# Loading the first four heads of Q and K in f32 through the SP and ACT queues and casting them on the chip

## The chip, the cores and the metric

The kernel runs on one core of one Trainium2 chip. The metric is device time in microseconds (us), the median of several executions of one compiled program. All repeated runs quoted here were undisturbed ("fast").

The names used below are these. PE (or TensorE) does matmuls, PEld is its weight load, DVE is VectorE, ACT is ScalarE, POOL is GpSimd, and SP is SyncE. A DMA that Pool issues can cast f32 to bf16 on the way ("Pool's queue"). A DMA issued by SP or ACT goes through a hardware queue and, in this kernel, brings f32, which an engine must cast afterwards.

## The reference

Attention with a squared ReLU (8 batches, 12 heads, 448 positions, head size 64), then RMS norm and a SwiGLU feed-forward layer over 3584 tokens (768 to 1536 to 768).

```python
def _attn_ref(q, k, v):                       # each (8, 12, 448, 64), f32
    scores = np.matmul(q, k.transpose(0, 1, 3, 2)) / np.sqrt(64)
    attn = np.maximum(scores, 0.0) ** 2 / 448
    return np.matmul(attn, v)

def _moe_ref(x, w_gate, w_val, w_out, rms_g): # x: (3584, 768)
    xn = x / np.sqrt(np.mean(x * x, axis=-1, keepdims=True) + 1e-06) * rms_g
    g = xn @ w_gate
    return (g / (1.0 + np.exp(-g)) * (xn @ w_val)) @ w_out
```

## The kernel before

The kernel is written by its own planner. While the program is built, `Planner` keeps a rough model of each engine's clock and of the DMA landings. At each step it emits whatever it believes can start next. What results is a fixed order of instructions for each engine, and each engine executes its list in order. Waits on real data are correct however wrong the model was; only the order is frozen.

Q and K have to be transposed on TensorE before the scores (tile `psT`). They come from DRAM by Pool's queue, four heads at a time; a DMA moves two chunks of Q, or one of two halves of K:

```python
def load_q(b, h0, h1, c0=0, c1=NCH):
    t = new_ld("q", b)                                  # bf16
    def go():
        nc.gpsimd.dma_start(out=t[:, h0:h1, c0*D:c1*D], in_=q[b, h0:h1].rearrange(...))
    landed("q", b, h0, h1, issue(go, ...))              # issue(): the planner's model of the DMA
...
def load_k(b, h0, h1):
    load_runs("k", b, h0, h1, low, 0, UH)               # partitions 0..63, 1024 B of f32 each
    load_runs("k", b, h0, h1, high, UH, U)              # partitions 64..127, 768 B each
```

The order of loads at the start:

```python
nc.scalar.preload_act_table_set(NORM_SET)
nc.sync.dma_start(out=g_sb[:], in_=moe_rms_g.rearrange("(kt p) -> p kt", p=P))
load_q(0, 0, 4, 0, 2)
load_k(0, 0, 4)
identTok = pl.task(-1, {"pool": 550.0}, lambda e: masks.make_identity(nc, ident[:]) and None)
load_q(0, 4, 8, 0, 2)
load_k(0, 4, 8)
load_v(0, 0, 4)
load_q(0, 8, H, 0, 2)
load_k(0, 8, H)
load_v(0, 4, H)
load_q(0, 0, H, 2, 4)
load_w(0, 2)                                            # first gate and value weights
...
```

Where the planner believes that PE has nothing to do for over 250 ns before the feed-forward part begins, it emits a filler: a matmul of constants into a bank that nobody reads (`psB`). The first ones warm TensorE up: in the profile of the kernel before they start 187 ns apart at first and 96 ns apart from about 5.5 us on.

```python
if self.warm() and (not times or min(times) > t + 250.0):
    return t, self.filler
...
def fill():
    ...
    nc.tensor.matmul(out=bank.fill, lhsT=ones_bf[:], rhs=busy_bf[:], start=True, stop=True)
    cost = 96.0 if max(pl.t) > pl.WARM else 189.0
```

Of the kernel before, what the change touches and what calls it, by code (L numbers as in the profile page):

```python
# [13 lines left out]
NCH = 4  # L14
U = 7
# [39 lines left out]
class Planner:  # L55
# [6 lines left out]
    def __init__(self, nc, tc, banks, wide, warm):  # L62
        self.nc, self.tc, self.banks, self.wide, self.warm = nc, tc, banks, wide, warm
        self.free = {"act": 1300.0, "dve": 1500.0, "pool": 1300.0, "sp": 1300.0}
        self.tasks, self.seq = [], 0
        self.t = [1100.0, 1100.0]
        self.mode = "row"
        self.ins = [[], []]
        self.aux = None
        self.cur, self.next0, self.q8 = None, [], []  # L70
        self.stream = []
        self.units, self.auxes, self.sneaks = [], [], []
        self.behind = mybir.DependencyInfo(
            mybir.DependencyClass.Sync, mybir.DependencyReason.DATA
        )
# [8 lines left out]
    def engine_next(self):  # L84
        best = None
        for item in self.tasks:
            prio, seq, cost, emit, need, out, then = item
            r = latest(need)
            if r is None:
                continue  # L90
            for e in cost:
                s = max(r, self.free[e])
                if e == "pool" and len(cost) > 1:
                    s += self.SLOW
                key = (s, prio, seq)
                if best is None or key < best[0]:
                    best = (key, item, e, s)
        return best
# [234 lines left out]
def kernel(  # L333
# [24 lines left out]
    PE_T = 2  # L358
    R = 14
    PACE = 0.93  # L360

    ctx.enter_context(tc.manual_schedule())

# [4 lines left out]
    apool = ctx.enter_context(tc.tile_pool(name="attn", bufs=R))  # L368
    xpool = ctx.enter_context(tc.tile_pool(name="xT", bufs=2))
    npool = ctx.enter_context(tc.tile_pool(name="norm", bufs=1))  # L370
    hpool = ctx.enter_context(tc.tile_pool(name="hT", bufs=1))
    spool = ctx.enter_context(tc.tile_pool(name="sig", bufs=3))
    opool = ctx.enter_context(tc.tile_pool(name="ostage", bufs=3))
    psum = ctx.enter_context(tc.tile_pool(name="psum", bufs=1, space=bass.MemoryType.PSUM))

    early = ExitStack()
    psum_x = early.enter_context(tc.tile_pool(name="psum_x", bufs=1, space=bass.MemoryType.PSUM))
# [6 lines left out]
    def act_cost(n, per=0.8333):  # L384
        return 172.0 + per * n

    def dve_cost(n, per=1.0417):
        return 156.0 + per * n
# [45 lines left out]
    def new_ld(nm, b):  # L434
        if (nm, b) not in ld:
            n, w = (PC, NCH) if nm == "q" else (P, UH)
            runs = nm == "v" or b < PE_T
            shape = [n, H, w * D] if runs else [n, w, H * D]
            ld[nm, b] = ldpool.tile(shape, BF16, name=nm + "b", tag=nm + "b")
            if nm == "k" and runs:  # L440
                nc.vector.memset(ld[nm, b][D:, :, (UH - 1) * D :], 0.0)
            ldtok[nm, b] = {}
        return ld[nm, b]

# [108 lines left out]
    def transposes(b, pairs, c0, c1, with_k, gate=lambda: True):  # L553
# [24 lines left out]
        def run(s):  # L578
# [18 lines left out]
            def copy(e):  # L597
                if with_k:
                    dst = t[:, pairs[0]].rearrange("p t s -> p (t s)")[:, c0 * PC : c0 * PC + width]
                    src = ps[:, :width]  # L600
                else:
                    dst = t[:, pairs[0] : pairs[-1] + 1, 1, c0 * PC : c1 * PC]
                    src = ps[:, :width].rearrange("p (j s) -> p j s", s=n)
                if e == "dve":
                    nc.vector.tensor_copy(out=dst, in_=src)
                else:
                    nc.scalar.copy(out=dst, in_=src)

            pl.task(
                2, {"dve": dve_cost(width, 0.52), "act": act_cost(width)}, copy, [Tok(end + 200.0)],  # L610
                done, free_bank(bank),
            )
            return end

        pl.auxes.append(Aux("transposes", "col", ready, run))

# [152 lines left out]
    def visit_aux(sub, k, then, after):  # L769
# [36 lines left out]
        def run(s):  # L806
# [38 lines left out]
            sub.visited = k + 1  # L845
            if (b, 0) not in xTs:
                xTs[b, 0] = xpool.tile([P, KT, S], BF16, name="xT", tag="xT")
                if b == 0:
                    x2s[b] = npool.tile([P, KT, S], BF16, name="x2", tag="x2")
                else:  # L850
                    accs[b] = npool.tile([P, S], FP32, name="acc", tag="acc")
                    x2s[b] = npool.tile([P, S], BF16, name="ssum", tag="ssum", bufs=2)
# [6 lines left out]
                else:  # L859
                    nc.vector.tensor_scalar_mul(out=xT[at], in0=ps[:, :, :n], scalar1=inv_attn)  # L860

            c = pl.task(1, {"act": act_cost(2 * n), "dve": dve_cost(2 * n)}, copy, [told], None, free_bank(bank))
            if b == 0:
                def squared(e):
                    nc.vector.tensor_tensor(out=x2s[b][at], in0=xT[at], in1=xT[at], op=ALU.mult)

# [45 lines left out]
    def norm_sum(sub):  # L912

        b, n, got = sub.b, sub.n, {}

        def ready():
            r, f = latest([sub.sum]), bank_ready()
            return None if r is None or f is None else max(r, f)

        def half(h):  # L920
            prt = (low, high)[h]
            if h:
                pl.wait_for(got["mm"])
            got["mm"] = nc.tensor.matmul(  # L924
                out=got["tile"][:, :n], lhsT=ones_bf[prt], rhs=x2s[b][prt], start=h == 0, stop=h == 1,
            ).ins

        def run():
            got["bank"] = take_bank()
            got["tile"] = got["bank"].take("psSS")  # L930

            def first(t):
                pl.ins[1].append((n, lambda: half(1), lambda t: norm_scale(sub, got, t), t - pl.PSUM + pl.HAND))

            pl.ins[0].append((n, lambda: half(0), first, 0.0))

        return Aux("sums", "row", ready, run)

    def norm_scale(sub, bk, ready):
# [5 lines left out]
        table["now"] = "silu"  # L945

        def power(e):
            if switch:
                nc.scalar.preload_act_table_set(NORM_SET)
            nc.scalar.activation(  # L950
# [12 lines left out]
        )]  # L963
        for kt in range(KT):
            def scale(e, kt=kt):
                if b not in xns:
                    xns[b] = npool.tile([P, KT, S], BF16, name="xn", tag="xn")
                xn = xns[b]
# [41 lines left out]
    def ffn_seg(sublist, w_nm, fbs):  # L1010
# [13 lines left out]
        def done(bk, ready):  # L1024
# [11 lines left out]
            else:  # L1036
                o = (b % 2) * S + q0

                def hidden(e):
                    if b // 2 not in hTs:  # L1040
                        hTs[b // 2] = hpool.tile([P, FT, 2 * S], BF16, name="hT", tag="hT")
                    h = hTs[b // 2]
                    s = sil[b, q0, fbs[0]][0]
                    nc.vector.tensor_tensor(  # L1044
# [108 lines left out]



    nc.scalar.preload_act_table_set(NORM_SET)
    nc.sync.dma_start(out=g_sb[:], in_=moe_rms_g.rearrange("(kt p) -> p kt", p=P))

    load_q(0, 0, 4, 0, 2)
    load_k(0, 0, 4)  # L1160
    identTok = pl.task(-1, {"pool": 550.0}, lambda e: masks.make_identity(nc, ident[:]) and None)
    load_q(0, 4, 8, 0, 2)
    load_k(0, 4, 8)
    load_v(0, 0, 4)
    load_q(0, 8, H, 0, 2)
    load_k(0, 8, H)
    load_v(0, 4, H)
    load_q(0, 0, H, 2, 4)
    load_w(0, 2)
    load_w(2, 4)  # L1170
# [16 lines left out]

    for j in range(HP):
        transposes(0, [j], 0, 2, True)
    for j in range(0, HP, 3):  # L1190
        transposes(0, [j, j + 1, j + 2], 2, 4, False, gate=lambda: begun(a0) >= 6)
    for j in range(HP):
        transposes(
            1, [j], 0, 4, True,
            gate=lambda j=j: begun(a1) >= 6 if j < 2 else begun(subs[2]) >= 3 * (j - 2),
        )


    period = 2 * FT * KT * (S / 2.4 + 2.5)

    def due_of(sub, i, total):
        if not sub.pace:
            return lambda: True

# [124 lines left out]
```

## Time and profile before

| | before |
|---|---|
| time, median (first three runs) | 441.01 us (440.78 to 441.23) |
| first transposes start | 6.44 us |
| first gate matmul (`psg`) starts | 25.19 us |
| span of the profiled run | 438.5 us |

The page of the kernel before. The first line is busy time, share of the span and count by engine. The second and third are PE's busy tenths and the granted TensorE clock in 40 slices of the span. The last is the chain of waits that ended last, by engine.

```profile
PE 432.1 (99%) x5443; PEld 302.4 (69%) x5443; DVE 272.0 (62%) x444; ACT 246.0 (56%) x345; POOL 79.7 (18%) x100
PE   8999999999999999999999999999999999999996
PEclk9999999999999999999999999999999999999999
PE 94%; DVE 2%; DMA 1%; ACT 1%; POOL 1%; issue 1%; ACTq 0%; POOLq 0%
```

PE is busy almost throughout, so from some point on only less PE work could help. The first 25 us are different, as the timeline shows. Its columns are start, duration, engine, line, operation, tiles, shape and count; in brackets stands how long the engine had been idle and for what.

```profile
1.18 5.13 PE L1278 MATMUL psB<-busy_bf,ones_bf 128*128 128x224 bf16 x30 [1.18 <-DVE busy_bf L397]
1.31 0.84 POOL L454 DMA_DIRECT2D qb<-in_q_dram  x1 [0.86 <-POOLq L1313]
2.13 1.25 POOL L466 DMA_DIRECT2D kb<-in_k_dram  x2
...
6.44 0.41 PE L590 MATMUL psT<-ident,kb 128*64 128x128 bf16 x8
6.66 0.29 PE L590 MATMUL psT<-ident,qb 112*64 112x112 bf16 x4
...
25.19 0.73 PE L139 MATMUL psg<-xn,wg_sb 64*128 64x224 bf16 x6
```

TensorE runs 30 fillers until Q and K have come, the transposes start at 6.44 us, and eight of them take 0.41 us.

The DMA view of the first 12 us, in slices of 0.3 us; an issue line ends with the size and the us from the start of the issue to the landing (the median, where it stands for several).

```profile
GB/s 0 0 0 0 0 0 3 5 3 22 49 112 157 149 182 144 150 78 107 106 159 120 132 141 114 139 106 111 115 134 152 164 172 167 162 171 178 173 183 160
qb<-in_q_dram POOLq DMA_DIRECT2D x3, 112.0 KB, 4.5
kb<-in_k_dram POOLq DMA_DIRECT2D x3, 128.0 KB, 4.5
kb<-in_k_dram POOLq DMA_DIRECT2D x3, 96.0 KB, 4.4
g_sb<-in_moe_rms_g_dram SPq DMA_DIRECT2D x1, 3.0 KB, 2.2
```

Pool's loads take about 4.5 us from issue to landing, as the median of three; the first ones, of heads 0 to 3, took 3.6 us (issued at 1.31 us, landed at 4.95). The only load on a hardware queue, 3 KB of norm weights, takes 2.2 us. That difference is what the change hopes to use.

### The profile page before, as it was taken

Reading aid. Unit: us, or ns where it says so; the run is one execution under the profiler, and the core shown is the slowest. Engines: PE = TensorE matmul, PEld = TensorE weight load, DVE = VectorE, ACT = ScalarE, POOL = GpSimd, SP = SyncE. Lnnn points to the kernel's source line nnn. Section 1 sums busy time; section 2 is a strip of 40 time slices with the busy share of each in tenths; the row PEclk is TensorE's granted clock in tenths of the full one; section 3 lists DMA queues with packets and bytes.
Section 4 is the critical chain, followed back from the end, with each engine's and each line's share of the span. In section 5 each row is a group of like instructions: output and inputs, shape, how many; then the busy total and the mean of one; then the engine's idle time right before and its main releaser. Section 6 shows DMA issues by size and latency. Waiting matters only on the chain.

```text
span 438.5 us, 12267 instructions
## 1 busy us (share of the span) xinstructions
PE 432.1 (99%) x5443; PEld 302.4 (69%) x5443; DVE 272.0 (62%) x444; ACT 246.0 (56%) x345; POOL 79.7 (18%) x100
## 2 busy tenths in 40 slices
PE   8999999999999999999999999999999999999996
PEld 6678878866569755774579855775569955676696
DVE  3799786439973676677844678577754677442200
ACT  4787575537754575656743576567744567342221
POOL 8643403291243000700043000100000000000000
PEclk9999999999999999999999999999999999999999
DMA  9999999999999950999049950652003200020023
GB/s 99 187 196 204 201 198 131 169 208 157 136 96 198 177 58 2 109 194 97 1 45 204 176 83 1 85 130 59 1 19 92 73 1 1 1 73 1 2 73 108
DMA packets 134052, 44.44 MB, mean 101 GB/s; under 512 B 105776, under 2 KB 130544, under 8 KB 134000
## 3 DMA queue, kind: packets, MB, share of 16 engines
q0 software_dynamic: 94624, 24.39, 58.6%
q1 hardware_dynamic: 39344, 19.27, 24.2%
q8 instruction: 42, 0.69, 0.7%
q14 instruction: 10, 0.08, 0.1%
q10 hardware_dynamic: 32, 0.01, 0.0%
HBM read 48.76 MB, written 11.01 MB: 136 GB/s over the span
## 4 chain that ended last, share of the span: by engine, by line
PE 94%; DVE 2%; DMA 1%; ACT 1%; POOL 1%; issue 1%; ACTq 0%; POOLq 0%
PE psO L139 26%; PE psg L139 25%; PE psv L139 25%; PE psAV L829 9%; PE psS L722 6%; PE psR L743 1%; PE psT L590 1%; DMA kb<-in_k_dram 1%; DVE r L675 1%; PE psB L1278 1%; DVE hT L1044 0%; DVE xT L860 0%; POOL qb L454 0%; PE psSS L924 0%; POOL kb L466 0%
## 5 line engine op out<-in xcount | busy, mean ns | idle before, releaser
L139 PE MATMUL psg<-xn,wg_sb 64*128 64x448 bf16 (+1 forms) x1296 | 173.6, 329 | 0.1
L139 PE MATMUL psv<-xn,wv_sb 64*128 64x448 bf16 (+1 forms) x1296 | 171.2, 328 | 0.0
L139 PE MATMUL psO<-wo_sb,hT 64*128 64x384 bf16 (+3 forms) x1368 | 134.3, 320 | 0.5 <-DVE hT L1044 0.5
L669 ACT ACTIVATE r<-psS 128x896 bf16<-128x896 f32 x122 | 109.0, 920 | 37.6 <-PE psS L722 36.5
L139 PEld LDWEIGHTS <-wg_sb 64*128 64x128 bf16 x1296 | 92.2, 94 | 36.8 <-issue 3.3
L139 PEld LDWEIGHTS <-hT 64*128 64x128 bf16 x1368 | 103.2, 94 | 19.3 <-issue 2.5
L139 PEld LDWEIGHTS <-wv_sb 64*128 64x128 bf16 x1296 | 90.2, 94 | 35.8 <-issue 3.0
L675 DVE TENSOR_TENSOR r<-r 128x896 bf16<-128x896 bf16 (+1 forms) x171 | 99.7, 610 | 17.8 <-ACT r L669 17.1
L1044 DVE TENSOR_TENSOR hT<-sil,psv 128x448 bf16<-128x448 bf16 x96 | 59.3, 617 | 56.1 <-PE psv L139 56.1
L1031 ACT ACTIVATE sil<-psg 128x448 bf16<-128x448 f32 x96 | 52.3, 545 | 47.7 <-PE psg L139 47.6
L722 PE MATMUL psS<-qkT 64*128 64x448 bf16 (+1 forms) x324 | 56.8, 329 | 0.6 <-ACT r L669 0.2
L1122 ACT COPY ost<-psO 128x384 f32<-128x384 f32 (+3 forms) x49 | 23.2, 473 | 52.9 <-PE psO L139 52.7
L829 PE MATMUL psAV<-r,vb 64*64 64x448 bf16 (+1 forms) x756 | 43.4, 335 | 0.3
L860 DVE TENSOR_SCALAR xT<-psAV 128x896 bf16<-128x896 f32 (+1 forms) x21 | 21.5, 1025 | 27.8 <-PE psAV L829 27.8
L496 POOL DMA_DIRECT2D kb<-in_k_dram x42 | 31.9, 809 | 36.2 <-DMA qkT<-kb 15.3
L466 POOL DMA_DIRECT2D vb<-in_v_dram x18 | 13.9, 826 | 133.3 <-PE psO L139 80.0
L669 ACT ACTIVATE r<-psR 128x896 bf16<-128x896 f32 (+1 forms) x24 | 20.9, 870 | 27.3 <-PE psR L743 27.2
L969 DVE SCALAR_TENSOR_TENSOR xn<-xT,g_sb,rstd 128x448 bf16<-128x448 bf16 (+1 forms) x54 | 30.2, 626 | 6.0 <-ACT rstd L954 5.9
L829 PEld LDWEIGHTS <-vb 64*64 64x64 bf16 x756 | 18.5, 105 | 20.4 <-PE psAV L829 8.2
L667 DVE TENSOR_SCALAR r<-psS 128x896 bf16<-128x896 f32 x22 | 23.9, 1087 | 13.2 <-PE psS L722 13.1
L722 PEld LDWEIGHTS <-qkT 64*128 64x128 bf16 x324 | 20.5, 94 | 11.3 <-issue 1.5
L877 DVE TENSOR_TENSOR x2f<-xT 128x896 f32<-128x896 bf16 x16 | 17.4, 1084 | 2.0 <-ACT xT L858 2.0
(44 smaller groups left out, 177.1 us busy)
## 6 DMA issues: line engine op xcount, KB each, us to landing
vb<-in_v_dram POOLq DMA_DIRECT2D x14, 384.0 KB, 8.8
kb<-in_k_dram POOLq DMA_DIRECT2D x45, 96.0 KB, 8.7
qb<-in_q_dram POOLq DMA_DIRECT2D x6, 672.0 KB, 16.4
out_dram<-ost SPq DMA_DIRECT2D x7, 336.0 KB, 4.3
wo_sb<-in_moe_w_out_dram POOLq DMA_DIRECT2D x2, 1152.0 KB, 21.9
out_dram<-ost SPq DMA_DIRECT2D x8, 288.0 KB, 3.8
out_dram<-ost SPq DMA_DIRECT2D x8, 240.0 KB, 4.4
wg_sb<-in_moe_w_gate_dram POOLq DMA_DIRECT2D x4, 384.0 KB, 12.6
```

Of the source, the lines that this page charges most:

```text
L139: mm = self.nc.tensor.matmul(out=seg.bank["tile"][:, off : off + seg.w], lhsT=lhsT[prt], rhs=rhs[prt], start=(seg.first and h == 0 and i = ...
L496: lambda o=o, i=i: nc.gpsimd.dma_start(out=o, in_=i),
L667: nc.vector.tensor_relu(out=r[:, :, :w], in_=ps[:, :, :w])
L669: nc.scalar.activation(out=r[:, :, :w], in_=ps[:, :, :w], func=ACT.Relu)
L675: eng.tensor_tensor(out=r[:, :, :w], in0=r[:, :, :w], in1=r[:, :, :w], op=ALU.mult)
L722: nc.tensor.matmul(out=ps[:, hh, o : o + n], lhsT=t[prt, j, 0, c * P : (c + 1) * P], rhs=t[prt, j, 1, sub.q0 : sub.q0 + n], start=True, st ...
L829: mm = nc.tensor.matmul(out=ps[hh * D : (hh + 1) * D, jj, :n], lhsT=vt[prt, 2 * (ja + jj) + hh, u * D : (u + 1) * D], rhs=r[prt, hh, o : o ...
L860: nc.vector.tensor_scalar_mul(out=xT[at], in0=ps[:, :, :n], scalar1=inv_attn)
L969: nc.vector.scalar_tensor_tensor(out=xn[:, kt, q0 : q0 + n], in0=xTs[b, 0][:, kt, q0 : q0 + n], scalar=g_sb[:, kt : kt + 1], in1=rstd[:, q ...
L1031: nc.scalar.activation(out=s[:, :m], in_=ps[:, :m], func=ACT.Silu)
L1044: nc.vector.tensor_tensor(out=h[:, fbs[0] : fbs[-1] + 1, o : o + n], in0=s[:, :m].rearrange("p (f s) -> p f s", s=n), in1=ps[:, :m].rearra ...
L1122: nc.scalar.copy(out=ost[:, c0 : c0 + w], in_=ps[:, :w])
```

## The change

Intent: have Q and K of the first four heads on the chip earlier, by way of two queues that are idle at the start. Pool can then begin with heads 4 to 7, and V comes in three loads instead of two. The diff, cut to what acts (switches that are set to change nothing are left out):

```diff
+    HF = 4
+    qf = fpool.tile([PC, HF, 2 * D], FP32, name="qf", tag="qf")
+    kf = fpool.tile([P, HF, UH * D], FP32, name="kf", tag="kf")
+    nc.vector.memset(kf[D:, :, (UH - 1) * D :], 0.0)
+    for h, queue in ((0, nc.sync), (2, nc.scalar)):
+        hs = slice(h, h + 2)
+        kv = k[0, hs].rearrange("h (p u) d -> p h (u d)", p=D)
+        queue.dma_start(out=qf[:, hs], in_=q[0, hs].rearrange(...)[:, :, : 2 * D])
+        queue.dma_start(out=kf[low, hs], in_=kv[:, :, : UH * D])
+        queue.dma_start(out=kf[high, hs, : (U - UH) * D], in_=kv[:, :, UH * D :])
     nc.scalar.preload_act_table_set(NORM_SET)
-    nc.sync.dma_start(out=g_sb[:], in_=moe_rms_g.rearrange("(kt p) -> p kt", p=P))
-    load_q(0, 0, 4, 0, 2)
-    load_k(0, 0, 4)
+    dma["t"] = 3700.0
+    pl.free["act"] = 3400.0
+    def cast(nm, h, at): ...            # ACT or DVE, f32 -> bf16, two heads; the planner believes
+                                        # that it can start at `at`
+    for h, at in ((0, 4100.0), (2, 5100.0)):
+        for nm in ("k", "q"):
+            new_ld(nm, 0)
+            landed(nm, 0, h, h + 2, cast(nm, h, at))
     identTok = ...
     load_q(0, 4, 8, 0, 2)
...
-    load_v(0, 4, H)
+    load_v(0, 4, 8)
+    load_v(0, 8, H)
...
     # transposes of batch 1
-            gate=lambda j=j: begun(a1) >= 6 if j < 2 else begun(subs[2]) >= 3 * (j - 2),
+            gate: a1.visited >= 1 if j < 2 else begun(subs[2]) >= 3 * j - 3
     # scores of batch 1 are "due" only after the third visit of a1 (DUE1)
```

The norm weights `g_sb` are loaded later, by SP. The four casts are planned for 4.1 and 5.1 us; this is the model that freezes the order.

More of the change, by code (lines that the diff above doesn't have):

```diff
@@ L65, in __init__ @@
         self.tasks, self.seq = [], 0
+        self.reserve = {e: 1e9 for e in self.free}
         self.t = [1100.0, 1100.0]
@@ L92, in engine_next @@
                 s = max(r, self.free[e])
+                if prio >= 2 and s + cost[e] > self.reserve[e] + 150.0:
+                    continue
                 if e == "pool" and len(cost) > 1:
@@ L360 @@
     PACE = 0.93
+    GATE = 1
+    LEAD = 3
+    WIDE_T = 0
+    DUE1 = 1
+    OLDSQ = 1
+    CHAINS = range(0, 0)
     ctx.enter_context(tc.manual_schedule())
@@ L370 @@
     npool = ctx.enter_context(tc.tile_pool(name="norm", bufs=1))
-    hpool = ctx.enter_context(tc.tile_pool(name="hT", bufs=1))
     spool = ctx.enter_context(tc.tile_pool(name="sig", bufs=3))
@@ L374 @@
     psum = ctx.enter_context(tc.tile_pool(name="psum", bufs=1, space=bass.MemoryType.PSUM))
+    staging = ExitStack()
+    fpool = staging.enter_context(tc.tile_pool(name="f32", bufs=1))
+    late = {}
     early = ExitStack()
@@ L440, in new_ld @@
             if nm == "k" and runs:
-                nc.vector.memset(ld[nm, b][D:, :, (UH - 1) * D :], 0.0)
+                nc.vector.memset(ld[nm, b][D:, b == 0 and 4 or 0 :, (UH - 1) * D :], 0.0)
             ldtok[nm, b] = {}
@@ L604, in copy @@
                 if e == "dve":
-                    nc.vector.tensor_copy(out=dst, in_=src)
+                    copied[b, pairs[-1]] = nc.vector.tensor_copy(out=dst, in_=src)
                 else:
-                    nc.scalar.copy(out=dst, in_=src)
+                    copied[b, pairs[-1]] = nc.scalar.copy(out=dst, in_=src)
             pl.task(
@@ L613, in run, with transposes_wide, ready, over @@
             return end
+        pl.auxes.append(Aux("transposes", "col", ready, run))
+    def transposes_wide(b, ja, gate):
+        done = [Tok(), Tok()]
+        toks = [identTok]
+        for i, j in enumerate((ja, ja + 1)):
+            kTok[b, j] = done[i]
+            for c in range(NCH):
+                qTok[b, j, c] = done[i]
+            for hh in range(2):
+                toks += ldtok["k", b][2 * j + hh] + ldtok["q", b][2 * j + hh]
+        def ready():
+            if not gate():
+                return None
+            r, f = latest(toks), wide_ready(1)
+            return None if r is None or f is None else max(r, f)
+        def run(s):
+            bank = take_wide()
+            ps = bank.take("psT", BF16, [P, 2, 1024])
+            t = new_qkT(b)
+            left = [2]
+            def over(t):
+                left[0] -= 1
+                if not left[0]:
+                    bank.free = t + 60.0
+            for i, j in enumerate((ja, ja + 1)):
+                steps = [("k", c, P, c * P) for c in range(UH)]
+                steps += [("q", c, PC, S + c * PC) for c in range(NCH)]
+                for nm, c, w, o in steps:
+                    for hh in range(2):
+                        nc.tensor.transpose(
+                            out=ps[hh * D : (hh + 1) * D, i, o : o + w],
+                            in_=ld[nm, b][:w, 2 * j + hh, c * D : (c + 1) * D],
+                            identity=ident[:w, :w],
+                        )
+                s += 56.0 * len(steps)
+                def copy(e, i=i, j=j):
+                    dst = t[:, j].rearrange("p t s -> p (t s)")
+                    (nc.vector.tensor_copy if e == "dve" else nc.scalar.copy)(out=dst, in_=ps[:, i, : 2 * S])
+                pl.task(
+                    2, {"dve": dve_cost(2 * S, 0.52), "act": act_cost(2 * S)}, copy,
+                    [Tok(s + 200.0)], done[i], over,
+                )
+            return s
         pl.auxes.append(Aux("transposes", "col", ready, run))
@@ L847, in run @@
                 xTs[b, 0] = xpool.tile([P, KT, S], BF16, name="xT", tag="xT")
-                if b == 0:
+                if b < OLDSQ:
                     x2s[b] = npool.tile([P, KT, S], BF16, name="x2", tag="x2")
@@ L860, in copy, with over @@
                     nc.vector.tensor_scalar_mul(out=xT[at], in0=ps[:, :, :n], scalar1=inv_attn)
-            c = pl.task(1, {"act": act_cost(2 * n), "dve": dve_cost(2 * n)}, copy, [told], None, free_bank(bank))
-            if b == 0:
+            def over(t):
+                bank.free = t + 60.0
+                if k == HP // 2 - 1 and b in CHAINS:
+                    pl.reserve["act"] = t + 1100.0 if b == 0 else 1e9
+            c = pl.task(1, {"act": act_cost(2 * n), "dve": dve_cost(2 * n)}, copy, [told], None, over)
+            if b < OLDSQ:
                 def squared(e):
@@ L914, in norm_sum, with half, put @@
         b, n, got = sub.b, sub.n, {}
+        parts = [x2s[b][:, i, :] for i in range(KT)] if b < OLDSQ else [x2s[b][:]]
         def ready():
-            r, f = latest([sub.sum]), bank_ready()
+            r, f = latest(sub.x2 if b < OLDSQ else [sub.sum]), bank_ready()
             return None if r is None or f is None else max(r, f)
-        def half(h):
+        def half(h, i):
             prt = (low, high)[h]
-            if h:
+            if h and not i:
                 pl.wait_for(got["mm"])
             got["mm"] = nc.tensor.matmul(
-                out=got["tile"][:, :n], lhsT=ones_bf[prt], rhs=x2s[b][prt], start=h == 0, stop=h == 1,
+                out=got["tile"][:, :n], lhsT=ones_bf[prt], rhs=parts[i][prt],
+                start=h + i == 0, stop=h == 1 and i == len(parts) - 1,
             ).ins
+        def put(h, after, cb):
+            for i in range(len(parts)):
+                pl.ins[h].append((n, lambda i=i: half(h, i), cb if i == len(parts) - 1 else None, after))
         def run():
@@ L930, in run @@
             got["tile"] = got["bank"].take("psSS")
-            def first(t):
-                pl.ins[1].append((n, lambda: half(1), lambda t: norm_scale(sub, got, t), t - pl.PSUM + pl.HAND))
-            pl.ins[0].append((n, lambda: half(0), first, 0.0))
+            put(0, 0.0, lambda t: put(1, t - pl.PSUM + pl.HAND, lambda t: norm_scale(sub, got, t)))
         return Aux("sums", "row", ready, run)
@@ L947, in power @@
         def power(e):
+            pl.reserve["act"] = 1e9
+            if b in CHAINS:
+                pl.reserve["dve"] = pl.free["act"] + 135.0 - 1283.0
             if switch:
@@ L965, in scale @@
             def scale(e, kt=kt):
+                pl.reserve["dve"] = 1e9
                 if b not in xns:
@@ L1039, in hidden @@
                 def hidden(e):
+                    if not late:
+                        staging.close()
+                        late["hT"] = ctx.enter_context(tc.tile_pool(name="hT", bufs=1))
                     if b // 2 not in hTs:
-                        hTs[b // 2] = hpool.tile([P, FT, 2 * S], BF16, name="hT", tag="hT")
+                        hTs[b // 2] = late["hT"].tile([P, FT, 2 * S], BF16, name="hT", tag="hT")
                     h = hTs[b // 2]
@@ L1152, in store, with cast, go, load_g @@
             pl.task(0, {"sp": 800.0}, send, [tok] if tail else osts[key][1])
-    nc.scalar.preload_act_table_set(NORM_SET)
-    nc.sync.dma_start(out=g_sb[:], in_=moe_rms_g.rearrange("(kt p) -> p kt", p=P))
-    load_q(0, 0, 4, 0, 2)
-    load_k(0, 0, 4)
+    HF = 4
[5 more added lines that the diff above has]
+        kv = k[0, hs].rearrange("h (p u) d -> p h (u d)", p=D)
+        queue.dma_start(
+            out=qf[:, hs], in_=q[0, hs].rearrange("h (p u) d -> p h (u d)", p=PC)[:, :, : 2 * D]
+        )
+        queue.dma_start(out=kf[low, hs], in_=kv[:, :, : UH * D])
+        queue.dma_start(out=kf[high, hs, : (U - UH) * D], in_=kv[:, :, UH * D :])
+    nc.scalar.preload_act_table_set(NORM_SET)
+    dma["t"] = 3700.0
+    pl.free["act"] = 3400.0
+    def cast(nm, h, at):
+        hs, src = slice(h, h + 2), {"q": qf, "k": kf}[nm]
+        n = 2 * src.shape[2]
+        def go(e):
+            to = new_ld(nm, 0)[:, hs, : src.shape[2]]
+            if e == "act":
+                nc.scalar.copy(out=to, in_=src[:, hs])
+            else:
+                nc.vector.tensor_copy(out=to, in_=src[:, hs])
+        return pl.task(0, {"act": act_cost(n, 0.9), "dve": dve_cost(n, 0.52)}, go, [Tok(at)])
+    for h, at in ((0, 4100.0), (2, 5100.0)):
+        for nm in ("k", "q"):
+            new_ld(nm, 0)
+            landed(nm, 0, h, h + 2, cast(nm, h, at))
+    def load_g(e):
+        pl.tc.add_manual_dep(nc.sync.nop().ins, copied[0, HP - 1].ins.name, pl.behind)
+        nc.sync.dma_start(out=g_sb[:], in_=moe_rms_g.rearrange("(kt p) -> p kt", p=P))
+    copied = {}
     identTok = pl.task(-1, {"pool": 550.0}, lambda e: masks.make_identity(nc, ident[:]) and None)
@@ L1189, with gate @@
         transposes(0, [j], 0, 2, True)
+    pl.task(0, {"sp": 500.0}, load_g, [kTok[0, HP - 1]])
     for j in range(0, HP, 3):
         transposes(0, [j, j + 1, j + 2], 2, 4, False, gate=lambda: begun(a0) >= 6)
-    for j in range(HP):
-        transposes(
-            1, [j], 0, 4, True,
-            gate=lambda j=j: begun(a1) >= 6 if j < 2 else begun(subs[2]) >= 3 * (j - 2),
-        )
+    for j in range(0, HP, 1 + WIDE_T):
+        def gate(j=j):
+            return getattr(a1, "visited", 0) >= GATE if j < 2 else begun(subs[2]) >= 3 * j - LEAD
+        if WIDE_T:
+            transposes_wide(1, j, gate)
+        else:
+            transposes(1, [j], 0, 4, True, gate)
     period = 2 * FT * KT * (S / 2.4 + 2.5)
     def due_of(sub, i, total):
+        if sub.b == 1 and DUE1:
+            return lambda: getattr(a1, "visited", 0) >= HP // 2
         if not sub.pace:
```

## The prediction

> **What bounds the kernel now.** The page gives TensorE 432 of 438.5 us busy at full clock; the chain of waits is 94% PE. But the first part is not real work. The timeline shows 77 filler matmuls (psB): 30 from 1.2 to 6.3 us, 47 more until 24.5 us. The first transposes start at 6.41 us, the first gate matmul (psg) at 25.19 us. Counting each matmul's columns at 2.4 GHz, halved or quartered for 64-row and 64*64 tiles, I get 392 us of useful PE work in the trace. By 26 us only 8.2 us of it is done: PE lags 17.8 us. The lag is 23.5 us at 60 us and then grows by about 5% of the time. So only the first 60 us can gain, mostly the first 26.
>
> In that stretch Pool issues the first Q at 1.31 us (0.84 us), then K in two parts (0.63 us each); they land at 4.95, 5.73 and 6.30 us. Heads 4 to 7 are issued from 3.91 us and land at 9.64 us, which the chain shows (DMA kb, 4.42 us). DMA moves 100 to 170 GB/s until 14 us, about 195 after that: early on issuing limits, later the DMA engines. From 10 to 40 us DVE and ACT are 70 to 97% busy.
>
> **What the change does.** It removes three Pool issues and moves 688 KB to six DMAs on the queues of SP and ACT, issued from about 0.74 us (the one such load of before took 0.47 us to issue and landed 2.2 us after its start; Pool's first took 3.6 us). It adds four casts (estimated 0.6 us on ACT, 0.3 on DVE, from similar copies) on engines that are idle then. Pool's stream begins about 2 us earlier. The Trainium skill ("Trainium Kernel Development and Optimization", Key Constraints) says that DMAs of all queues share the same 16 engines and that several queues save issue time only. That fits the trace: until 14 us there is spare bandwidth, afterwards none, so weights can land only 1 to 2 us earlier.
>
> The first cast should start near 4.5 us and the first transposes near 5.2 us: 1.2 us earlier.
>
> The order of instructions changes: 18 fillers before the first transposes instead of 30, but 63 instead of 47 between them and the first psg, with the same 7.7 us of useful work. 16 more fillers at 94 ns cost 1.5 us, if they don't merely fill waits. DVE does more before xn (6 against 4 rectified tiles, 15 against 12 squares). So I expect the first psg hardly earlier, about 24.5 us, but DVE further ahead, so less waiting from 26 to 40 us. Batch 1's scores start later (after 18 us of useful work instead of 15). From about 100 us of useful work on, the order is the same.
>
> **Sum.** -1.2 us at the start, +0.3 for more fillers than waits, -0.6 from DVE's work done ahead: about -1.5 us, 439.5 us, 8 in 10 within 437.5 to 441.3. Faster by over 2%: 0.01; within 2%: 0.98; slower by over 2%: 0.01.
>
> **What would show it.** First transposes at 4.8 to 5.7 us; K of heads 4 to 7 landed by about 8.2 us; the first weights near 19 us instead of 20.6; first psg at 24 to 25 us; lag at 60 us about 22.
>
> **What would make it wrong.** The hardware queues' loads and Pool's fight for the engines and the first cast slips past 6 us; fillers planned for earlier data delay PE; the gain is lost because weights bind PE between 26 and 60 us; or the better start removes most waits and gains over 3 us.

The useful PE work was counted by the columns of each matmul, at one fixed rate. The 392 us and the lags are estimates by that count; what the trace shows is 224 columns in 96 ns for a filler at full pace.

## The result, and the profile after

| | before | after |
|---|---|---|
| median of 6 runs each | 440.88 us (440.44 to 441.23) | 443.95 us (443.55 to 445.24) |
| first transposes | 6.44 us | 8.40 us |
| first `psg` | 25.19 us | 29.11 us |
| span of the profiled run | 438.5 us | 442.1 us |

The ratio is 1.0074, 95% interval 1.006 to 1.0088. A ratio here is the mean time of one kernel's fast runs over that of the other's of the same rounds, so it is not quite the ratio of the medians. The change made the kernel 0.7% slower, 3.1 us by the medians.

The same lines of the page after:

```profile
PE 433.0 (98%) x5447; PEld 302.4 (68%) x5447; DVE 271.9 (61%) x446; ACT 247.3 (56%) x348; POOL 79.0 (18%) x99
PE   5999999999999999999999999999999999999996
PEclk9999999999999999999999999999999999999998
PE 96%; DMA 1%; DVE 1%; ACT 1%; SPq 0%; issue 0%; ACTq 0%
```

In PE's line only the first slice differs: 5 instead of 8. The timeline after:

```profile
0.74 0.38 SPq L1242 DMA_DIRECT2D qf<-in_q_dram  x1
1.18 0.74 SPq L1245 DMA_DIRECT2D kf<-in_k_dram  x1
1.18 3.52 PE L1397 MATMUL psB<-busy_bf,ones_bf 128*128 128x224 bf16 x18 [1.18 <-DVE busy_bf L408]
1.49 0.85 POOL L465 DMA_DIRECT2D qb<-in_q_dram  x1 [0.19 <-issue]
1.96 0.85 SPq L1246 DMA_DIRECT2D kf<-in_k_dram  x1
3.23 0.67 DVE L1260 CAST qb<-qf 112x256 bf16<-112x256 f32 x2 [1.04 <-DMA qf<-in_q_dram]
7.73 1.14 ACT L1258 CAST kb<-kf 128x512 bf16<-128x512 f32 x2 [3.88 <-DMA kf<-in_k_dram]
8.40 0.64 PE L601 MATMUL psT<-ident,kb 128*64 128x128 bf16 x8 [3.71 <-ACT kb L1258]
8.83 0.40 PE L601 MATMUL psT<-ident,qb 112*64 112x112 bf16 x4
...
29.11 0.27 PE L142 MATMUL psg<-xn,wg_sb 64*128 64x224 bf16 x1
```

There are two findings. Q came as hoped and was cast at 3.23 us. K did not: ACT stood idle for 3.88 us waiting for it, began the cast at 7.73 us instead of the planned 4.1 us, and PE stood idle for 3.71 us behind that. And when PE began, the same eight transposes took 0.64 us instead of 0.41.

The DMA view of the first 12 us after:

```profile
GB/s 0 0 0 0 0 5 65 164 330 205 137 31 31 134 234 249 223 230 266 234 223 213 197 194 189 195 188 199 173 177 176 196 186 186 193 196 189 193 193 195
kf<-in_k_dram SPq DMA_DIRECT2D x1, 128.0 KB, 5.0
kf<-in_k_dram ACTq DMA_DIRECT2D x1, 128.0 KB, 4.8
qf<-in_q_dram SPq DMA_DIRECT2D x1, 112.0 KB, 2.5
qf<-in_q_dram ACTq DMA_DIRECT2D x1, 112.0 KB, 2.6
kf<-in_k_dram ACTq DMA_DIRECT2D x1, 96.0 KB, 4.8
kf<-in_k_dram SPq DMA_DIRECT2D x1, 96.0 KB, 5.7
```

The DMA first in each queue landed after 2.5 and 2.6 us. The second and third took 4.8 to 5.7 us, so the last K of heads 0 and 1 was there at 1.96 + 5.7 = 7.6 us. Between 3.3 and 3.9 us the DMA engines moved only 31 GB/s although the K loads had been issued: there is a hole where the load should have been fastest. The queues in these 0.6 us (packets, MB, share of the 16 engines' time):

```profile
q10 hardware_dynamic: 14, 0.01, 18.3%
q1 hardware_dynamic: 6, 0.01, 2.9%
```

Only the two hardware queues moved anything, 20 packets; Pool's queue (q0 in other windows) is not in the list. So in the hole the DMA engines were neither full nor taken by Pool's data, although Pool had issued its first load at 1.49 us. (These GB/s count bytes as written, so a Pool load with cast counts half of what it reads.)

Adding up from the timelines: first transposes +1.96 us; from there to the first `psg` 20.71 us instead of 18.75, again +1.96 us; from `psg` to the end 413.0 us instead of 413.3, so -0.3 us. The sum is the 3.6 us by which the profiled spans differ. All of the loss is made before 29.11 us.

### The profile page after: what moved, and what is told of

It is laid out like the page before. It is cut to its first block, busy times and chain, and to the rows that moved or that the text cites. A ratio compares the mean times of both kernels' runs of the same rounds, so it can differ in the third digit from the quotient of the medians.

```text
span 442.1 us, 12293 instructions
## 1 busy us (share of the span) xinstructions
PE 433.0 (98%) x5447; PEld 302.4 (68%) x5447; DVE 271.9 (61%) x446; ACT 247.3 (56%) x348; POOL 79.0 (18%) x99
## 4 chain that ended last, share of the span: by engine, by line
PE 96%; DMA 1%; DVE 1%; ACT 1%; SPq 0%; issue 0%; ACTq 0%
PE psO L142 26%; PE psv L142 25%; PE psg L142 25%; PE psAV L892 9%; PE psS L785 7%; PE psT L601 2%; DMA kf<-in_k_dram 1%; PE psR L806 1%; PE psB L1397 1%; DVE r L738 0%; DVE r L730 0%; PE psSS L994 0%; ACT r L732 0%; SPq L1245 0%; PE psSS L1070 0%; ACT qkT L618 0%
## 5 line engine op out<-in xcount | busy, mean ns | idle before, releaser
L142 PEld LDWEIGHTS <-wv_sb 64*128 64x128 bf16 x1296 | 88.9, 94 | 36.1 <-issue 3.2
L785 PE MATMUL psS<-qkT 64*128 64x448 bf16 (+1 forms) x324 | 55.9, 332 | 0.1
L477 POOL DMA_DIRECT2D vb<-in_v_dram x20 | 14.9, 776 | 134.6 <-PE psO L142 95.4
```

What stands on the lines that cost most here:

```text
L142: mm = self.nc.tensor.matmul(out=seg.bank["tile"][:, off : off + seg.w], lhsT=lhsT[prt], rhs=rhs[prt], start=(seg.first and h == 0 and i = ...
L785: nc.tensor.matmul(out=ps[:, hh, o : o + n], lhsT=t[prt, j, 0, c * P : (c + 1) * P], rhs=t[prt, j, 1, sub.q0 : sub.q0 + n], start=True, st ...
```

## The experiments

Theory 1: K lands late, and because the order is fixed, that lateness goes through to the end. Theory 2, its addition: TensorE, left idle, runs slowly for some us (the "slow pace"), which costs as much again. Rivals: the new gates of batch 1; V in three loads; the order with its extra fillers.

### Undo one part: the gates (a_old_gates)

```diff
-            return getattr(a1, "visited", 0) >= GATE if j < 2 else begun(subs[2]) >= 3 * j - LEAD
+            return begun(a1) >= 6 if j < 2 else begun(subs[2]) >= 3 * (j - 2)
-    DUE1 = 1
+    DUE1 = 0
```

> The changed kernel with the gates of batch 1's transposes and scores put back as they were; the new loads stay. Theory 1 (the hardware queues' K lands at 6.0 to 7.6 us, so the transposes start at 8.4 us, and the fixed order with its fillers shifts as a whole): no change, 443.5 to 444.5 us, first transposes at 8.4 and first psg at about 29 us. Rival (the reordering by the gates costs the time): back to 440.5 to 441.5 us.

Measured: 444.09 us (443.18 to 444.50), ratio to before 1.0071 (1.0056 to 1.0086). The gates are not the cause. In the profiled run the first transposes start at 8.18 us and the first `psg` at 28.48 us. Its trace also shows something that matters for theory 2:

```profile
8.18 0.41 PE L601 MATMUL psT<-ident,kb 128*64 128x128 bf16 x8 [3.49 <-ACT kb L1258]
...
9.11 0.64 PE L601 MATMUL psT<-ident,kb 128*64 128x128 bf16 x8
```

With the same 18 fillers and 3.49 us of idle time, the first transposes still ran at full pace; the slow pace began only at about 8.6 us and ended at about 12.1 us.

### Undo the other part: the loads (b_pool_loads)

The start of the kernel before (Pool loads heads 0 to 3 first, `g_sb` on SP at the start) in the changed kernel.

> The changed kernel with the first four heads of Q and K loaded by Pool as before, first in its queue; V in three loads and the new gates stay. Theory 1: 440.2 to 441.5 us, first transposes at 6.4 us, first psg near 25 us. Rival (the gates, or V in three loads): 443 to 444.5 us.

Measured: 440.44 us (440.10 to 440.62), ratio 0.999 (0.9975 to 1.0005), first transposes 6.63 us, first `psg` 25.38 us. The loss comes with the loads through the hardware queues, their casts and the order planned for them, which this run takes back together; the gates and V in three loads are free.

### Tell the planner the truth (c_true_plan)

```diff
-    for h, at in ((0, 4100.0), (2, 5100.0)):
+    for h, at in ((0, 7700.0), (2, 7700.0)):
-    pl.free["act"] = 3400.0
+    pl.free["act"] = 7700.0
```

> The changed kernel, but its planner is told that the casts can start at 7.7 us (measured) instead of 4.1 and 5.1 us; loads and gates stay. 40 fillers before the first transposes instead of 18. Theory 1, second half (part of the loss comes from an order that was planned for data at 4.1 us): K still lands at 6 to 7.6 us, first transposes at 8.4 us, but the clock is warm and psg comes by 27 us: 441.5 to 442.8 us. If the lateness of K alone costs the time, 443.5 to 444.5 us as changed.

Measured: 444.53 us (444.03 to 444.98), ratio 1.0083 (1.0068 to 1.0098): a miss, and just above the other expected range too. The transposes started warm at 8.41 us, but the planner, which takes the next thing that it believes ready, now put a fourth attention visit ahead of the first `psg`, which came only at 30.96 us. So this run does not separate the two causes; it says only that an honest start time did not mend this order.

### Keep TensorE busy while it waits (d_warm)

```diff
     def run(s):                                # of the first transposes
+        for _ in range(36):                    # not known to the planner
+            nc.tensor.matmul(out=fps[:, 0, :HALF], lhsT=ones_bf[:], rhs=busy_bf[:], start=True, stop=True)
```

> The changed kernel with 36 fillers more before the first transposes, not known to the planner, so that TensorE does not stand idle from 4.7 to 8.4 us; all else in the same order. In the changed kernel the first 24 transposes took 0.64 and 0.40 us a group where before they took 0.41 and 0.29. Theory: idle TensorE came back slow, which cost about 1 us: 442.8 to 443.4 us, and the groups take 0.41 and 0.29 us again. Rival (the slow groups are the profile's, or hidden by waits): 443.6 to 444.4 us.

Measured: 443.41 us (442.07 to 444.84), ratio 1.0063 (1.0033 to 1.0093). The groups were fast again:

```profile
9.27 0.41 PE L607 MATMUL psT<-ident,kb 128*64 128x128 bf16 x8
```

I had put in too many fillers: the transposes started 0.87 us later than in the changed kernel. Even so `psg` came 0.6 us earlier, at 28.52 us. From the first transposes to `psg` it took 19.25 us instead of 20.71, so the slow pace cost about 1.5 us in that stretch. The timed runs scatter too much to give the net of it.

### Take the fillers away (e_after_nofill, f_before_nofill)

In both kernels, no filler is emitted once transposes have begun; the plan still counts them.

> The changed kernel in the same order and plan, but the 63 fillers after the first transposes are not emitted. Theory (the plan put them where data should come late; as the real start is 3.9 us later than planned, most of them only delay real work): first psg 1.5 to 3 us earlier than 29.1 us, time 441.5 to 443 us. Rival (they fill waits for ACT and DVE, which remain): first psg and time unchanged within 0.7 us, or later if TensorE comes back slow after waits.

> Control: the kernel before, without its 47 fillers after the first transposes. If fillers cost time only where the start missed its plan: 440.5 to 441.3 us, first psg at 25.2 us. If fillers delay real work in any case: 1 to 2 us faster than before.

Measured: the changed kernel 446.33 us (445.38 to 448.37), ratio 1.0132 (1.0102 to 1.0161); the kernel before 442.03 us (441.51 to 444.75), ratio 1.0046 (1.0011 to 1.0081). Both theories fell; what came true is only the rival's last clause for the changed kernel, that TensorE comes back slow after waits. In the changed kernel `psg` did come earlier, at 28.16 us, but TensorE was then slow in the feed-forward part itself: eleven gate matmuls took 2.26 us, where the changed kernel has 1.21.

```profile
29.65 2.26 PE L142 MATMUL psg<-xn,wg_sb 64*128 64x224 bf16 x11
```

So the fillers are not what delays PE; without them more is lost.

### Who makes K late? (g_pool_late, h_one_queue, i_k_first; one look each)

A long memset of 4096 columns on Pool ahead of its loads:

> The changed kernel with a long memset on Pool ahead of its loads, so that the hardware queues load alone for some us. A diagnosis, slower on purpose. If Pool's loads in the same DMA engines delay K: all K of the first four heads landed by 4.5 us instead of 6.0 to 7.6. If the hardware queues are slow by themselves: K still lands at 5.5 us or later.

```profile
kf<-in_k_dram SPq DMA_DIRECT2D x1, 128.0 KB, 4.1
kf<-in_k_dram ACTq DMA_DIRECT2D x1, 128.0 KB, 3.8
kf<-in_k_dram SPq DMA_DIRECT2D x1, 96.0 KB, 3.7
```

With the hardware queues alone, K still needed 3.5 to 4.1 us. The last K landed at 5.6 us instead of 7.6. Pool's stream therefore accounts for about 2 us of the last landing, but alone the queues still do not reach the 4.5 us of the expectation. The transposes started at 6.41 us:

```profile
6.41 0.64 PE L601 MATMUL psT<-ident,kb 128*64 128x128 bf16 x8 [1.71 <-ACT kb L1258]
```

They were slow, up to about 16.4 us, and Pool's own loads were now late; the time was 443.82 us.

All six loads on SP's queue (`((0, nc.sync), (2, nc.sync))`):

> The changed kernel with all six hardware loads on SP's queue. If the two hardware queues hinder each other: heads 0 and 1 landed by 5 us, heads 2 and 3 at about 7.5 us. If Pool's loads or the K loads themselves are slow: heads 0 and 1 at 7 us or later as in the changed kernel, heads 2 and 3 later still (8.5 us).

Measured: 445.23 us. The low half of K of heads 0 and 1 landed at 4.1 us, its high half, third in the queue, at 6.7 us, the last of heads 2 and 3 at 9.4 us. This lies between the two expectations. The transposes of heads 0 and 1 even started 0.95 us earlier than in the changed kernel, at 7.45 us, but for the four heads together two queues are better than one.

K ahead of Q in each queue:

> The changed kernel with K ahead of Q in each hardware queue. If it is the second place in the queue that makes a load late: K at 4 to 4.5 us, Q at 6 to 7.5 us, first transposes again at 8 us. If it is K's own shape (64 partitions, 1024 and 768 bytes a piece): K again at 6 us or later, Q later still.

```profile
kf<-in_k_dram SPq DMA_DIRECT2D x1, 128.0 KB, 3.4
kf<-in_k_dram ACTq DMA_DIRECT2D x1, 128.0 KB, 2.9
kf<-in_k_dram ACTq DMA_DIRECT2D x1, 96.0 KB, 4.4
kf<-in_k_dram SPq DMA_DIRECT2D x1, 96.0 KB, 4.5
```

Measured: 443.74 us. The halves that are now first landed by 4.1 us, those second in the queue at 5.9 and 6.1 us, and Q, now third, at 7.6 and 7.8 us. The transposes of K started at 6.86 us, those of Q, which now waited, at 8.18 us. So K's shape is not what makes it late: as the first in its queue it took 2.9 and 3.4 us, and what stood behind it took 4.4 us or more. But the place in the queue alone does not decide either: in h_one_queue, with ACT's queue empty, the second DMA of SP's queue landed after 2.9 us (issued at 1.18 us, landed at 4.1), with Pool issuing as here. How Pool's stream and the second hardware queue share in the delay is not separated. With both queues in use, some load of these heads was late in either order.

### What on-time data would be worth (j_on_time)

A wrong result on purpose: all loads as in the change, but into tiles that nobody reads; the casts read zeros.

```diff
+    qg = fpool.tile([PC, HF, 2 * D], FP32, name="qg", tag="qg")      # the loads go here
+    kg = fpool.tile([P, HF, UH * D], FP32, name="kg", tag="kg")
+    nc.vector.memset(kf[:], 0.0)                                     # the casts read these
+    nc.vector.memset(qf[:], 0.0)
```

> A wrong result on purpose: the changed kernel in its own order, and with the same loads at the same times, but these land in tiles that nobody reads; the casts read zeros set on the chip. So K and Q of the first four heads are there on time. Theory (the lateness of K is the whole loss): first transposes by 5.2 us, first psg at 24.5 to 26 us, time 439.5 to 441 us. If the order or the traffic of the other loads costs too: first psg at 27 us or later and 442 us or more.

```profile
4.63 0.50 PE L601 MATMUL psT<-ident,kb 128*64 128x128 bf16 x8
...
8.10 0.41 PE L601 MATMUL psT<-ident,kb 128*64 128x128 bf16 x8 [0.94 <-DMA kb<-in_k_dram]
```

Measured: 440.68 us median (440.11, 440.26, 441.09, 444.56), ratio to before 1.0013 (0.9968 to 1.0057), first `psg` 24.74 us. In the profile and in three of the four runs the whole loss is gone, so no cost of the order or of the other traffic is shown; the run of 444.56 us makes the interval wide. But look at the gain: the transposes start 1.8 us earlier than before the change and `psg` only 0.45 us earlier. PE has run ahead to heads 4 to 7 and waits for them (0.94 us at 8.10 us). Even with the first four heads on time, no gain of this change is shown.

### Half the change (k_q_only, l_k_only)

Only Q on the hardware queues and Pool beginning with K (casts planned for 3.5 us); and only K on the hardware queues and Pool beginning with Q (casts planned for 4.5 us).

> Only Q of the first four heads goes through the hardware queues (in the changed kernel it landed at 3.2 and 3.4 us, ahead of K); Pool begins with K of these heads, 0.8 us earlier than before. V in three loads and the gates as in the change; planned for casts at 3.5 us. Theory (it was K, second in each hardware queue and met by Pool's traffic, that came late): K lands at 5.0 and 5.6 us, first transposes at about 5.7 us, 439.7 to 440.6 us. If hardware loads at the start slow Pool's stream as a whole: K after 6 us, 441 us or more.

> Only K of the first four heads goes through the hardware queues, first in each; Pool begins with Q of these heads. Planned for casts at 4.5 us. If K was late because Q went ahead of it: K lands by 4.5 us, first transposes at 5.2 us, 439.5 to 440.5 us. If K is late because Pool's traffic meets it: K lands at 5.5 to 6.5 us, first transposes near 6.8 us, 441.5 to 443 us.

Measured: only Q 441.39 us (439.84, 440.05, 442.73, 443.14), ratio 1.0023 (0.9987 to 1.0059); K from Pool at 5.0 and 5.6 us as expected, first transposes 5.73 us. Only K 440.38 us (439.73, 439.77, 441.00, 441.27), ratio 0.9989 (0.9969 to 1.0008); the last K at 5.5 and 5.7 us, which is the second expectation for the landing, but the first transposes already at 6.15 us. Both are the same as before within the intervals, with a larger scatter.

### The slow pace alone, and lateness alone, in the kernel before (m_before_cold, q_before_late)

These two make each suspected cause without any new load. The first emits only 18 of the 30 fillers ahead of the first transposes; the second adds 20.

> The kernel before with 18 instead of 30 fillers ahead of its first transposes, nothing else changed (the plan still counts them). TensorE then idles from about 4.7 to 6.4 us. Theory (an idle TensorE of over 1.6 us or so comes back slow, and that alone is a good part of the loss, as the late-Pool run with first transposes at 6.41 us and slow groups suggests): groups of eight transposes take 0.64 instead of 0.41 us, first psg after 26.5 us, time 442 to 443.5 us, or some runs at 441 and some at 443. Rival (only the late data count): 440.5 to 441.3 us.

> The kernel before with 20 fillers more ahead of its first transposes: TensorE starts them at about 8.4 us as in the changed kernel, but warm, and with all data there. Theory (a late start goes through to the end one to one, as TensorE is in order and its fillers are fixed): first psg at about 27.1 us, 442.2 to 443 us. Rival (waits later on take up part of it, as loads have not moved): first psg at 25.5 to 26.5 us, 441 to 442 us.

The fillers and what follows them in m_before_cold:

```profile
1.18 3.52 PE L1284 MATMUL psB<-busy_bf,ones_bf 128*128 128x224 bf16 x18 [1.18 <-DVE busy_bf L397]
6.50 0.41 PE L590 MATMUL psT<-ident,kb 128*64 128x128 bf16 x8 [1.80 <-DMA kb<-in_k_dram]
...
8.48 0.56 PE L722 MATMUL psS<-qkT 64*128 64x224 bf16 x4
...
10.24 0.64 PE L590 MATMUL psT<-ident,kb 128*64 128x128 bf16 x8
```

Measured: 441.73 us (440.96 to 443.62), ratio 1.0028 (1.0013 to 1.0042), about 1.2 us. The slow pace did not begin with the first transposes, as I had expected, but about 1.6 us after the idle time had ended, and first `psg` came at 26.17 us. The time lies between the two expected ranges, and the start of the transposes had moved by only 0.06 us. So leaving TensorE idle for 1.8 us is by itself worth about 1.2 us here. The six runs agree with it: five have a mean granted clock of 0.991 to 0.994 and take 441.53 us or more, and the one with 0.999 is the fastest, 440.96 us.

In q_before_late:

```profile
9.00 0.41 PE L596 MATMUL psT<-ident,kb 128*64 128x128 bf16 x8
...
27.75 0.73 PE L139 MATMUL psg<-xn,wg_sb 64*128 64x224 bf16 x6
```

Measured: 442.56 us (441.53 to 443.93), ratio 1.0042 (1.0027 to 1.0056), about 1.9 us. In the profiled run the start was 2.56 us late, the first `psg` 2.56 us late and the span 2.4 us longer. In this run the late start goes through nearly one to one, with the data long on the chip: nothing later takes it up. (Twenty fillers at 96 ns are 1.9 us; in the profiled run TensorE also reached its full pace later than before. The starts of the timed runs are not known.)

### The slow start taken away (n_kfirst_warm, o_konly_warm, p_qonly_warm)

The K-first, K-only and Q-only versions with 17, 13 and 8 more fillers ahead of the first transposes.

> The K-first version (first transposes at 6.86 us, slow groups, 443.7 us) with 17 more fillers ahead of the first transposes. Theory: groups at 0.41 us, first psg at 26.5 to 27.5 us, 441.5 to 442.5 us. Rival (slow groups don't matter): 443.3 to 444.2 us.

> A try at a version that beats both: only K of the first four heads on the hardware queues (that run had 439.7, 439.8, 441.0 and 441.3 us), with 13 fillers more ahead of the first transposes, so that a little jitter in the loads does not leave TensorE idle for over 1.5 us. If the higher times were slow starts of TensorE: all runs at 439.5 to 440.3 us. If not: again up to 441.3 us.

> The same with only Q on the hardware queues (439.8, 440.1, 442.7 and 443.1 us), 8 fillers more ahead of the first transposes. If the two higher times were slow starts of TensorE: all runs at 439.6 to 440.6 us. If not: again some near 443 us.

Measured: K first 442.59 us (441.82, 442.47, 442.72, 447.08), ratio 1.0065 (1.0029 to 1.01), 0.09 us above the expected range, against 443.74 us for the single look without the fillers. The profiled run is the one of 447.08 us, so its trace does not show the mended case. It shows something else: the second K of heads 0 and 1 landed 6.8 us after its issue, where the look before had 4.5 us. PE then idled for 1.62 us in spite of the fillers, and the slow pace ran from about 10.1 to 13.8 us.

```profile
kf<-in_k_dram SPq DMA_DIRECT2D x1, 96.0 KB, 6.8
```

K only: 440.07 us (439.71 to 440.96), ratio 0.999 (0.9978 to 1.0002). Its scatter became somewhat smaller, but two of the five runs still lie above the expected range (440.42 and 440.96 us). It is the best version that I ran, and it is not shown to beat the kernel before. Q only: 440.60 us (440.14 to 445.56), ratio 1.0023 (0.9989 to 1.0057). Three of six runs are within the expected range and a fourth is 0.07 us above it; what made the 445.56 us is not known, as that run has no trace. Its granted clock was 0.99 against 0.997 to 1.0 in the other five, so a slow stretch in spite of the fillers is possible.

## Why the prediction was wrong

- **The step that failed first: "The first cast should start near 4.5 us and the first transposes near 5.2 us: 1.2 us earlier."** The cast of K started at 7.73 us and the transposes at 8.40 us, 1.96 us later than before. I took the 2.2 us of a load that was alone in its queue and on idle DMA engines for all six loads. It held for the first DMA of each queue (2.5 and 2.6 us), and not for those behind it with Pool's stream running (4.8 to 5.7 us). With Pool held back they took 3.5 to 4.1 us. The term of -1.2 us was in truth about +2 us; q_before_late shows that such a term counts nearly in full.
- **A term that was missing:** idle TensorE. The prediction counted 18 fillers instead of 30 ahead of the transposes and saw only their cost. They bring TensorE to its full pace and keep it there. The slow pace alone cost 1.2 us in m_before_cold, and about 1.5 us from transposes to `psg` by d_warm's trace. Together with the late start, 2.0 + 1.2 = 3.2 us, against 3.1 us measured. I call the sum an agreement and not a proof: the two parts were measured in the kernel before, with an interval of about 0.6 us each way, and g_pool_late shows that they do not simply add when other loads move as well.
- **"+0.3 for more fillers than waits":** not contradicted. In d_warm, at full pace, the stretch to `psg` was 0.5 us longer than before. But my reason, that fillers delay PE, fell with e_after_nofill and f_before_nofill.
- **"-0.6 from DVE's work done ahead":** from `psg` to the end the changed kernel took 0.3 us less, and j_on_time 0.5 us more. No such gain is shown.
- **What held:** K of heads 4 to 7 was to land by about 8.2 us, and landed at 8.28; the first weights near 19 us, and they landed at 18.70 us. Pool's stream did move ahead. (The lag at 60 us was not measured after the change.) The prediction named the failure ("the hardware queues' loads and Pool's fight for the engines and the first cast slips past 6 us") but left it outside its range.
- **The Trainium skill** says in "DMA: Bandwidth & Descriptors", section "Issuing engines are not separate DMA queues", that DMAs of SP, ACT and Pool run on the same 16 engines and interleave, and that starting them from several engines saves only the issue time. The prediction used this for the weights and not for K, where it mattered: 7.6 us for the last K of heads 0 and 1 with Pool beside it, 5.6 us without. The trace agrees that they interleave: from 3.9 to 6 us Pool's queue moved 0.15 MB beside 0.17 and 0.15 MB of the two hardware queues. But in the hole just before, the engines were busy for about a fifth of the time, so sharing them is not the whole of the 2 us.
- It also says, in "TensorE: Matmul & The Clock Gate", section "What's actually happening", that TensorE runs at half its clock until it has been busy for about 3.4 us, and again after an idle window of about 3.4 us. The trace agrees in kind: 18 fillers took 3.52 us at the start, 187 ns from one to the next, against 96 ns at full pace, and after 3.71 us of idle time eight transposes took 0.64 us instead of 0.41. But the idle time alone does not tell when the slow pace comes. Two courses occur after the same 18 fillers. The trace files hold the changes of the granted clock: in the changed kernel's the first is the one to full, at 12.86 us, so its TensorE seems never to have been at full pace before. In a_old_gates it was full from 5.27 us, half from 8.68 and full again from 12.09 us. So the slow pace can be one that was never left or one that was fallen back to, and d_warm's trace gives the cost of the first, m_before_cold that of the second.

What stays open: what makes the hole of 31 GB/s between 3.3 and 3.9 us. In the same two slices the K-first look has 67 and 52 GB/s and j_on_time 96 and 65, while with Pool held back they have 229 and 312. So it comes with Pool's start; Pool's data did not yet move in it (see the queues above), and no run separates what else of Pool's start makes it. Open too is what lies behind single runs of 444 to 447 us, which came with loads on the hardware queues (j_on_time, n_kfirst_warm, p_qonly_warm) but also once without (f_before_nofill, 444.75 us). In each of these four series that run has the lowest granted clock (0.993, 0.995, 0.99 and 0.983), which points to a slow stretch of TensorE; only the one of n_kfirst_warm has a trace, and it shows one, beside the late K.

## What to carry to other kernels

Cost a load by its place in its queue and by what else starts beside it, not by the landing of a lone DMA: here the first in each queue landed in 2.5 us and the next two in 4.8 to 5.7 us. In a kernel whose order is frozen when it is built, a wait that the plan did not foresee can pass nearly one to one to the end, as it did here (2.56 us at the start, 2.4 us of the span). Pool's loads, done when the plan had them, beat hardware loads planned for 4.1 us and landed at 7.6; but telling the planner the later time did not mend this order. And ask first what the load is worth when it is on time: a run that fed the casts with zeros answered in one go that there was almost nothing to win: the next heads' loads were the next wait (0.94 us).

## What the Trainium skill lacked or had wrong

- "TensorE: Matmul & The Clock Gate", section "Why this matters for your kernels", asks for no idle gaps above about 3 us. Here an idle gap of 1.80 us, after 18 fillers, was enough: the slow pace began about 1.6 us after the gap had ended (0.56 us for four score matmuls that take 0.37), and cost about 1.2 us (ratio 1.0028). In n_kfirst_warm 1.62 us was enough, after 35 fillers. With 1.50 us of idle time in the profiled K-only run no slow stretch followed.
- The same page shows clock events in a trace, in its section "Seeing it yourself", and warns there that they have been unreliable. Here the recorded changes agree with the durations (m_before_cold: granted clock 0.57 between 8 and 12 us, where eight transposes took 0.64 us). What misleads is the time before the first recorded change: the profile of the changed kernel shows a granted clock of 9 tenths or more in every early slice, while matmuls took 1.5 times as long (0.64 against 0.41 us), as its first record is at 12.86 us. The page could say that up to the first change only the durations tell the pace.
- "DMA: Bandwidth & Descriptors" calls the hardware queues generally faster (section "Issuing engine by pattern") and gives about 0.6 us to the first byte against 1 us for Pool's (section "Specifications"). It has no figure for a second and third DMA behind the first while Pool starts its own: 4.8 to 5.7 us to landing here, against 2.5 and 2.6 us for the first and 3.5 to 4.1 us with Pool held back. In the kernel before, Pool's own first Q and K each took 3.6 us from issue to landing, so K was there at 5.7 and 6.3 us, earlier than by the hardware queues.
- None of the pages that I used gives the scatter of landings at the start of a kernel: the same K load took 4.5 us in one run and 6.8 us in another.
